# A table of places is changed in a fused two-layer FNet and Infini-attention kernel: natural scores, value products, key, query, value and output chains

## The chip, the cores and the metric

The kernel runs on one core of one Trainium2 chip. The metric is the device time of one execution in microseconds (us), lower is better. The times and the profile are of the whole program: one launch, all inputs and the output in the chip's memory.

Engines are named as the profile names them: PE is TensorE (matmuls; PEld its weight loads), DVE is VectorE, ACT is ScalarE, POOL is GpSimd, SP is SyncE, whose instruction queue issues nearly all the DMAs.

## The reference, cut to what matters

```
x = x + A(layernorm(x))      # A: y = Re(DFT_seq(DFT_hidden(x)))
x = x + B(layernorm(x))      # B: attention in 4 segments with a memory
x = x + A(layernorm(x))
x = x + B(layernorm(x))

# B, with S = 2048 rows, D = 512, 32 heads of 16, segments of L = 512 rows:
q, k, v = x@wq, x@wk, x@wv           # per head
for s in range(4):
    logits = q_s @ k_s.T * scale + mask       # causal in a segment
    a_dot  = softmax(logits) @ v_s
    a_mem  = (phi(q_s) @ M) / (phi(q_s) @ z + 1e-6)
    o_s    = g * a_mem + (1 - g) * a_dot
    M, z   = M + phi(k_s).T @ v_s, z + sum(phi(k_s))
return concat(o) @ wo
```

All numbers are float32; the matmuls of A and the projections of B split each operand into two float32r parts and add three products.

## The kernel before

The four layers follow each other with an overlap: the first layer A runs to about 373 us in the profile, its last step (`y`, the hidden DFT) to about 448 us, the first attention B from about 440 to 900 us, the second A to 1305 us, the second B to the end.

**A unit** of an attention is one segment and four heads; there are 32 in each attention, eight in a segment. A unit's work:

- `stack` loads a unit's queries and keys (`stkq`, `stkk`) by DMA. Two heads stand in the upper and two in the lower half of the 128 rows, so that a matmul of one half and one of the other run side by side.
- `natural_max` makes the scores row by row (`nat`, on PE), and DVE takes each row's maximum out of them (`junk<-nat`, `mx`). It has five steps: 512 columns for the first pair of heads, then 128 and 384, the same again for the second pair, and 256 twice for both. The last step writes the negated maxima (`mparts`).
- `max_rows` turns them over (`mT` on PE, `mt` on ACT) and a DMA puts them beside the queries.
- `softmax_values` makes the scores again, turned (`sT`, on PE), less the maximum, and ACT caps and exponentiates them (`sT<-sT`, `pT<-sT`). It has five steps as well: 256 columns twice, 384 and 128 twice, 512 twice.
- `value_products` multiplies with the values (`pv_bank`), ACT copies the sum (`ot`), and `output` turns it (`on`) and scales it on DVE (`rec`, `ot<-on`).

Between these stands **the chain**: the key, query, value and output projections (`pqk`, `pvv`, `po`) of the neighbouring segments, cut into half products of 64 rows (`half_product`). A tile of the chain takes 12 steps in the upper half of the rows, and 18 steps after its start (`LAGS`) 12 steps in the lower half, so that two tiles in a row overlap and most steps are a pair. A unit has 24 steps: 10, then 6, then 8, each such window spread over a part of the unit (`WIN`). The order of the tiles is a string (`ORDER` for the two middle segments, `ORDER_FIRST`, `ORDER_LAST`), two names for each unit, where `-` is none.

At a unit's head stand, in some units, the memory's reads (`mem_read`: `pm`, with `den` and `onat` on DVE) and updates (`mem_update`: `pkT`, copied by ACT as `pkn`, and `pM`, added up on DVE), the turns of the next segment's rows (`prep`: `xnT`), and of the attention's outputs (`transpose_out`: `oT`).

**What sets the order.** Nothing of this is ordered by a scheduler on PE. Each step is put at a place, a number: unit n begins at place t = t0 + 10n, and the tables say how far from t a step stands (`N_AT` for the natural scores, which run up to 16 places ahead, `S_AT` for the softmax, `PV` for the value products, `TURN` for `max_rows`, and `UPA`, `UPB`, `READ_AT` in units for the memory). All steps are sorted by their place, and PE's instructions keep that order. DVE, ACT, POOL and SP get theirs from the framework, which starts from the same order and knows priorities; the maxima have a high one.

All PE results go to eight banks of 512 numbers per row (`bank`). A new result takes the bank that has been free the longest, and its first matmul waits until DVE or ACT has emptied it.

The lines that the prediction speaks of:

```
1338  place(0, softmax_values(*unit(n)), [t + k for k in sorted(set(S_LAST if light_unit else S_AT))])
1343  place(1.9, max_rows(*unit(n)), [turn])
1344  place(1, natural_max(*unit(n)), [t + k for k in (N_LAST if light_nat else N_AT)])
1374  chain.update({at + h: tile for h, tile in enumerate(order) if tile})
1407          return t0 + SU * u + at + 1.8 * r / n
```

Of the kernel before, what the change touches and what calls it, by code (L numbers as in the profile page):

```python
# [27 lines left out]
LT = L // P  # L28
# [13 lines left out]
VW = DH + 1  # L42
HALF = NT // 2
URGENT = 150
S_AT = (1.0, 2.5, 3, 5.5, 7.5)
N_AT = (-16.05, -15.1, -12.05, -10.95, -8.0, -8)
PV = 11.9
PVF = 12
W = 2.5
TURN = -5  # L50
TO = 0.75
TURNED = (12.5, 12.5, 14)
WIN = ((4.1, 10), (6.1, 6), (8.1, 8))
LAGS = 18
ORDER = "k3 q3 o1 o0 o2 o3 k0 q0 v2 q1 k1 k2 v1 q2 v3 v0"
OT_AT = (1, 1, 1, 2)
PREP_AT = (2, 3)
READ_AT = (1, 3, 5, 7)
UPA = (-1, 3, 3, 7)
UPB = (4, 5, 6, 8)  # L60
ORDER_PRE = "q2 k2"
ORDER_FIRST = "q3 k3 - - - - v2 k0 q0 q1 k1 k2 v0 q2 v3 v1"
PREP_FIRST = (2, 3)
UPA_FIRST = (1, 2, 4, 5)
UPB_FIRST = (2, 7, 8, 8)
ORDER_LAST = "k3 q3 o2 o0 - o3 - o1 - - - - - - - -"
OT_LAST = (1, 2, 1, 1)
READ_LAST = (1, 3, 5, 6)
NL0 = 0
SL0 = 2  # L70
TURN_LAST = -5
TURNED_LAST = (12.5, 12.5, 14)
TO_LAST = 0.8
ROWS_AT = (-38, -24, -12, 2, 26, 28, 40, 66)
S_LAST = (1.5, 2.5, 3, 6.0, 6)
N_LAST = (-15.55, -14.05, -12.5, -11.0, -10.9, -8)
PV_LAST = 11.5
OWO = 0.8
OWU = 0.6
OWP = 0.4  # L80
OWR = 0.2
OWB = 0.3
STK = -21.5
TERMS = {
# [14 lines left out]
def spectral_infini_kernel(  # L99
# [151 lines left out]
    def place(order, gen, *at):  # L251
        for t in itertools.chain(*at):
            slots.setdefault(t, []).append((order, gen))

    def run_from(t, n, step=1):
        return range(t, t + n * step, step)
# [18 lines left out]
    def place_spectral(x_in, x_out, t0, end, ln_at, direct):  # L275
# [340 lines left out]
        def split_u(tcn, tt):  # L616
            sl = slice(tt * P, (tt + 1) * P)
            for cc in range(2):
                home = ("ut", 8) if (tcn, cc) == (TC - 1, 1) else ("w", 16)
                us[tcn, tt, cc] = t = pair("us", *home)  # L620
                for half in range(2):
                    hi, lo = (
                        t[:, h, half * 256 : (half + 1) * 256].rearrange("p (m s) -> p m s", s=P)
                        for h in range(2)
                    )
                    split(hi, lo, c[tcn, (half, cc)][:, :, sl])
            yield
# [72 lines left out]
        else:  # L700
# [25 lines left out]
            for tcns in (0, 1), (2, 3):  # L726
                at = {tcn: [] for tcn in tcns}
# [13 lines left out]
        for tcn in range(TC):  # L741
            if tcn == 0:
                at = [end + k // 2 for k in range(nh)]
            elif tcn < TC - 1:
                at = [end + nh // 2 + ((tcn - 1) * nh + k) // 3 for k in range(nh)]
            else:
                at = run_from(end + nh // 2 + 2 * nh // 3 + 1, 2 * DT, 2)
                at = [*at, *(at[-1] + 4 + k for k in range(LT))]
            for tt in range(LT):
                place(3.7, split_u(tcn, tt), [at[tt * 2 * DT if tcn < TC - 1 else 0] - 4])  # L750
            place(4, (hidden if tcn < TC - 1 else hidden_last)(tcn), at)

    def place_attention(x_in, x_out, t0, w_at, out_at):
# [241 lines left out]
        def max_rows(s, g, u):  # L995
            qs, parts = stacks[s, g, u, "q"], maxima.pop((s, g, u))
            n = MROWS * HU * LT
            mt = sb.tile([P, P], F32R, name="mt", bufs=2)
            for a in SIDES:
                at = slice(a, a + P // 2)  # L1000
                pt = bank("mT", (P, P // 2))
                T.transpose(pt[:MCOLS], parts[at].bitcast(F32), ident[at, at])
                with tc.high_priority(offset=URGENT):
                    A.activation(mt[:n, at], pt[:n], AF.Copy)
            for a, at in enumerate(SIDES):
                n = MROWS * HP * LT
                nc.sync.dma_start(
                    qs[at + KROWS : at + KROWS + MROWS].rearrange("p h s -> p (h s)").bitcast(F32),
                    mt[a * n : (a + 1) * n].bitcast(F32),
                )  # L1010
            yield

        def softmax_values(s, g, u):
# [57 lines left out]
            def ev(t, f):  # L1071
                events.setdefault(t, []).append(f)

            for p in range(HP):
# [13 lines left out]

                ev((S_LAST if (s, g * NU + u) >= (NSEG - 1, SL0) else S_AT)[3 + p], first)
                ev((S_LAST if (s, g * NU + u) >= (NSEG - 1, SL0) else S_AT)[1 + p], second)  # L1090
            p2 = []
# [6 lines left out]

            ev((S_LAST if (s, g * NU + u) >= (NSEG - 1, SL0) else S_AT)[0], third)

# [18 lines left out]
        def value_products(s, g, u):  # L1119
            pending.pop((s, g, u))()  # L1120
            yield
# [191 lines left out]
        def unit(n):  # L1313
            return n // USEG, n % USEG // NU, n % NU
# [15 lines left out]
        def apart(s, k):  # L1330
            return t0 + SS * s + SU * k + W

        for n in range(NSEG * USEG):
# [3 lines left out]
            final = n >= NSEG * USEG - 2  # L1337
            place(0, softmax_values(*unit(n)), [t + k for k in sorted(set(S_LAST if light_unit else S_AT))])
            place(0.9, value_products(*unit(n)), [t + (PVF if final else PV_LAST if light_unit else PV)])
            turned = t + (TURNED_LAST if light_unit else TURNED)[2 if n >= NSEG * USEG - 3 else n % USEG == USEG - 1]  # L1340
            place(TO_LAST if light_unit else TO, output(*unit(n)), [turned])
            turn = t - (6 if x_out is out_tiles and n == NSEG * USEG - 1 else -(TURN_LAST if light_nat else TURN))
            place(1.9, max_rows(*unit(n)), [turn])
            place(1, natural_max(*unit(n)), [t + k for k in (N_LAST if light_nat else N_AT)])
            place(0.6, stack(*unit(n)), [t + STK])
        for s in range(NSEG):
            b = t0 + SS * s
            for j in range(2):
                t = b - 43 + 5 * j if s == 0 else apart(s - 1, (PREP_AT if s > 1 else PREP_FIRST)[j])
                first = (11, 8, 5, 3) if s else (8, 5, 4, 3)  # L1350
                place(OWP, prep(s, (2 * j, 2 * j + 1)), [*(t - d for d in first), t, t + 1] if s == 0 else [*(t - d for d in first), t])
            if s == 0:
# [5 lines left out]
            for i in range(LT):  # L1358
                if s > 0:
                    place(OWO, transpose_out(s - 1, i), [apart(s, (OT_AT if s < NSEG - 1 else OT_LAST)[i])])  # L1360
            order = []
            for name in (ORDER_FIRST if s == 0 else ORDER if s < NSEG - 1 else ORDER_LAST).split():
                n, i = name[0], int(name[1:] or 0)
# [23 lines left out]
            for g in range(NG):  # L1387
# [9 lines left out]
                if s > 0:  # L1397
                    place(OWR, mem_read(s, g), [apart(s, (READ_AT if s < NSEG - 1 else READ_LAST)[g])] * 2)
                if s < NSEG - 1:
                    update = mem_update(s, g)  # L1400
                    place(OWU, update, [apart(s, (UPA if s else UPA_FIRST)[g])])
                    place(OWB, update, [apart(s, (UPB if s else UPB_FIRST)[g])])
        def chain_time(k):
# [23 lines left out]
    b2 = a2 + TC * 7 * HALF + LEAD  # L1427

    def w_at(b):
        return lambda k: b - 52 + 2 * k if k < 12 else b + 20 + 5 * (k - 12)  # L1430

    place_spectral(
        x_tiles, mids[0], a1, b1 - LEAD,
# [5 lines left out]
        mids[1], mids[2], a2, b2 - LEAD,  # L1439
        [((2 * j, 2 * j + 1), a2 + t) for j, t in enumerate(ROWS_AT)],  # L1440
        False,
# [87 lines left out]
```

## Time and profile before

| | us |
|---|---|
| time, median of 3 runs (lowest, highest) | 1762.76 (1760.72, 1765.97) |
| the profiled execution's own time | 1763.62 |
| its span, first to last instruction | 1761.5 |
| PE busy in the span | 1719.8 |
| DVE, ACT, POOL busy | 1315.4, 1092.1, 489.6 |

The profile is of one execution. A busy PE is not PE at its peak: matmuls are pipelined, their ends are modelled, and a gap of under 0.15 us counts as none. So the waits of PE are read from the starts of its rows in the timeline: two rows that stand next to each other without a wait start one matmul's length apart.

### The profile page before, as it was taken

How to read it: one execution, taken by the hardware profiler on the slowest of the kernel's cores; microseconds unless marked ns; L12 is line 12 of the kernel's file. 1: busy time of each engine (PE TensorE's matmuls, PEld its weight loads, DVE VectorE, ACT ScalarE, POOL GpSimd, SP SyncE). 2: the span in 40 equal slices, each digit the busy share in tenths (PEclk: the TensorE clock that was granted, in tenths of full speed). 3: DMA queues.
4: the chain of work that ended last, by engine and by line, in shares of the span. 5: the costliest groups of instructions: out<-in, count | busy, mean ns of one | idle time of the engine just before them, and what ended most of it. 6: DMA issues, size and time to landing. Idle time of an engine off the chain costs nothing.

```text
span 1761.5 us, 35311 instructions
## 1 busy us (share of the span) xinstructions
PE 1719.8 (98%) x11504; PEld 1347.1 (76%) x11504; DVE 1315.4 (75%) x3939; ACT 1092.1 (62%) x2452; POOL 489.6 (28%) x767
## 2 busy tenths in 40 slices
PE   8999999999999999999999999999999999999998
PEld 6888777878677787777678878888876777778775
DVE  8888977873676876878978997667647668677785
ACT  3344443532489788788774566444318887887885
POOL 1000000004237455455410000000034454753542
PEclk9999999999999999999999999999999999999999
DMA  8787774355356454555657767653545555545551
GB/s 283 246 271 236 241 258 163 107 175 176 111 148 163 129 155 110 163 155 149 176 186 227 262 224 243 193 171 117 179 150 155 130 128 158 152 122 155 143 143 34
DMA packets 145510, 303.28 MB, mean 172 GB/s; under 512 B 18096, under 2 KB 22192, under 8 KB 145328
## 3 DMA queue, kind: packets, MB, share of 16 engines
q1 hardware_dynamic: 138416, 288.44, 55.3%
q10 hardware_dynamic: 6912, 12.59, 1.9%
q8 instruction: 93, 1.52, 0.4%
q14 instruction: 89, 0.73, 0.1%
HBM read 211.83 MB, written 88.08 MB: 170 GB/s over the span
## 4 chain that ended last, share of the span: by engine, by line
PE 79%; DVE 10%; ACT 4%; DMA 3%; issue 3%; POOL 0%; SPq 0%; DVEq 0%; ACTq 0%; POOLq 0%
PE m L125 25%; PE pqk L125 9%; PE y L125 8%; PE pv_bank L125 8%; PE nat L125 6%; PE u L125 5%; PE pvv L125 5%; PE po L125 5%; PE sT L125 4%; DVE junk L969 2%; DVE c L592 2%; DVE clo L142 1%; PE pM L125 1%; ACT pT L1043 1%; PE pm L125 1%
## 5 line engine op out<-in xcount | busy, mean ns | idle before, releaser
L969 DVE CUSTOM_DVE_ANT_0 junk<-nat,mask 128x128 bf16<-128x128 f32 (+3 forms) x896 | 368.7, 457 | 226.2 <-PE nat L125 214.2
L1043 ACT ACTIVATE pT<-sT 128x512 f32<-128x512 f32 x640 | 352.2, 608 | 2.5 <-DVE sT L1038 1.3
L125 PE MATMUL m<-chi,xa 128*128 128x512 f32 x1056 | 308.2, 392 | 2.4 <-DVE c L592 2.1
L1046 POOL TENSOR_SCALAR_AFFINE_SELECT pT<-pT 128x256 f32<-128x256 f32 (+1 forms) x448 | 192.3, 443 | 336.5 <-ACT pT L1043 298.7
L125 PE MATMUL m<-clo,xa 128*128 128x512 f32 x720 | 231.3, 393 | 5.0 <-DVE clo L142 4.7
L125 PEld LDWEIGHTS m<-chi,xa 128*128 128x128 f32 x1056 | 198.1, 189 | 46.5 <-DVE c L592 2.9
L1040 ACT ACTIVATE sT<-sT 128x256 f32<-128x256 f32 x625 | 180.0, 329 | 72.3 <-PE sT L125 63.9
L125 PE MATMUL nat<-stkk,stkq 48*128 48x384 f32 (+3 forms) x1024 | 195.3, 356 | 8.6 <-PE sT L125 3.1
L125 PE MATMUL pqk<-xT,wq 64*128 64x512 f32 (+1 forms) x720 | 194.1, 402 | 0.8 <-ACT pT L1043 0.6
L125 PE MATMUL pqk<-xT,wk 64*128 64x512 f32 (+1 forms) x720 | 193.8, 398 | 0.2
L125 PE MATMUL y<-wdt,us 128*128 128x512 f32 x768 | 182.4, 391 | 0.2 <-DVE wdt L142 0.2
L125 PE MATMUL pvv<-wv,xT 64*128 64x512 f32 (+1 forms) x672 | 175.1, 402 | 0.6 <-DVE xT L142 0.6
L125 PEld LDWEIGHTS nat<-stkk,stkq 48*128 48x128 f32 x1024 | 123.5, 189 | 60.7 <-ACT pT L1043 19.3
L125 PEld LDWEIGHTS y<-wdt,us 128*128 128x128 f32 x768 | 143.5, 188 | 30.5 <-DVE wdt L142 0.9
L125 PE MATMUL pv_bank<-pT,v_all 128*32 128x512 f32 (+3 forms) x2048 | 164.1, 453 | 0.6 <-DVE xr L236 0.6
L125 PE MATMUL sT<-stkq,stkk 50*128 50x256 f32 (+3 forms) x1024 | 163.2, 332 | 1.1 <-DVE mx L969 0.4
L125 PEld LDWEIGHTS m<-clo,xa 128*128 128x128 f32 x720 | 135.1, 188 | 38.0 <-DVE clo L142 9.4
L211 POOL TENSOR_TENSOR r<-ve,half_neg 128x4 f32<-128x4 f32 (+2 forms) x22 | 20.8, 945 | 510.4 <-DVE ve L209 486.5
L140 ACT ACTIVATE chi<-cring 128x512 fp32r<-128x512 f32 (+1 forms) x138 | 99.7, 728 | 89.5 <-PE m L125 42.4
L125 PE MATMUL po<-wo,oh 64*128 64x512 f32 (+1 forms) x672 | 145.9, 398 | 1.3 <-ACT oh L140 0.5
L125 PEld LDWEIGHTS pqk<-xT,wq 64*128 64x128 f32 (+1 forms) x720 | 125.8, 190 | 12.9 <-issue 1.5
L125 PEld LDWEIGHTS pqk<-xT,wk 64*128 64x128 f32 (+1 forms) x720 | 122.8, 186 | 12.2 <-issue 2.2
(191 smaller groups left out, 3124.3 us busy)
## 6 DMA issues: line engine op xcount, KB each, us to landing
cring<-in_ct SPq DMA_DIRECT2D x97, 256.0 KB
scrk<-parts SPq DMA_DIRECT2D x96, 256.0 KB
stkq<-scrq SPq DMA_DIRECT2D x128, 192.0 KB
stkk<-scrk SPq DMA_DIRECT2D x128, 192.0 KB
cring<-sum SPq DMA_DIRECT2D x95, 256.0 KB
xt<-mid SPq DMA_DIRECT2D x64, 256.0 KB
scrq<-parts SPq DMA_DIRECT2D x32, 512.0 KB
cring<-in_ct SPq DMA_DIRECT2D x27, 512.0 KB
```

What stands on the lines that cost most here:

```text
L125: return tc.keep_in_program_order(op(*args, **kwargs))
L140: pin(A.activation(hi, src, AF.Copy, scale=scale))
L142: lo_engine.tensor_tensor(out=lo, in0=src, in1=hi.bitcast(F32), op=ALU.subtract)
L211: G.tensor_tensor(out=r, in0=ve, in1=half_neg[:, :n], op=ALU.pow)
L592: V.tensor_tensor(out=dst, in0=c[tcn, base][:, m], in1=ps[m], op=op)
L969: last_max[0] = V.tensor_tensor_reduce(trash, src, mask[:, 512 - n :], 1.0, 3e38, ALU.add, ALU.min, dst,)
L1040: done = A.activation(blocks, blocks, AF.Relu)
L1043: A.activation(dst[a], ps, AF.Exp, scale=-SCALE)
L1046: G.affine_select(blocks, blocks, pattern=[[0, n] for n in blocks.shape[1:-1]] + [[1, P]], compare_op=ALU.is_ge, fill=0.0, base=0, channel ...
```

## The change

The change is in constants and in two expressions that now read theirs from constants. `N_AT` puts the first two natural steps a place later, `S_AT` and `PV` the first softmax step and the value products half a place sooner, `READ_AT`, `UPA`, `UPB` the memory's reads and updates to other units; `ORDER` exchanges the first two tiles and the order of the values; `ORDER_LAST` and `READ_LAST` put the last segment's output tiles elsewhere; `WO` and `WOS` place the loads of the output weights; `ROWS_AT` those of the second layer A's rows. `MDELAY` is 4, as it was.

```
-S_AT = (1.0, 2.5, 3, 5.5, 7.5)
-N_AT = (-16.05, -15.1, -12.05, -10.95, -8.0, -8)
-PV = 11.9
+S_AT = (0.5, 2.5, 3, 5.5, 7.5)
+N_AT = (-15.05, -14.15, -12.0, -10.95, -8.0, -8)
+PV = 11.5
-TO = 0.75
+TO = 0.7
-ORDER = "k3 q3 o1 o0 o2 o3 k0 q0 v2 q1 k1 k2 v1 q2 v3 v0"
+ORDER = "q3 k3 o1 o0 o2 o3 k0 q0 v1 q1 k1 k2 v2 q2 v0 v3"
-READ_AT = (1, 3, 5, 7)
-UPA = (-1, 3, 3, 7)
-UPB = (4, 5, 6, 8)
+READ_AT = (1, 2, 5, 7)
+UPA = (1, 3, 3, 6)
+UPB = (3, 4, 6, 8)
-UPA_FIRST = (1, 2, 4, 5)
-UPB_FIRST = (2, 7, 8, 8)
-ORDER_LAST = "k3 q3 o2 o0 - o3 - o1 - - - - - - - -"
+UPA_FIRST = (1, 1, 3, 5)
+UPB_FIRST = (2, 8, 8, 7)
+ORDER_LAST = "k3 q3 o0 o2 - - - o1 - o3 - - - - - -"
-READ_LAST = (1, 3, 5, 6)
+READ_LAST = (1, 1, 5, 6)
+MDELAY = 4
+WO = 25
+WOS = 4
-ROWS_AT = (-38, -24, -12, 2, 26, 28, 40, 66)
-S_LAST = (1.5, 2.5, 3, 6.0, 6)
-N_LAST = (-15.55, -14.05, -12.5, -11.0, -10.9, -8)
+ROWS_AT = (-38, -26, -18, 2, 26, 26, 40, 66)
+S_LAST = (1.5, 2.5, 3, 5.5, 6)
+N_LAST = (-15.05, -14.55, -12.0, -11.0, -10.9, -8)
-OWO = 0.8
+OWO = 0.85
-OWP = 0.4
-OWR = 0.2
+OWP = 0.3
+OWR = 0.1
...
-                at = [*at, *(at[-1] + 4 + k for k in range(LT))]
+                at = [*at, *(at[-1] + MDELAY + k for k in range(LT))]
...
-        return lambda k: b - 52 + 2 * k if k < 12 else b + 20 + 5 * (k - 12)
+        return lambda k: b - 52 + 2 * k if k < 12 else b + WO + WOS * (k - 12)
```

What PE gets of it in a unit of a middle segment, before. It is the first attention's unit that starts at 597.8 us in the profile, whose chain is outputs alone (`po`); rows with x10 are five pairs:

```order
L125 MATMUL sT<-stkq,stkk 128x384 x2
L125 MATMUL sT<-stkq,stkk 128x128 x2
L125 MATMUL nat<-stkk,stkq 128x512 x2
L125 MATMUL po<-wo,oh 128x512 x10
L125 MATMUL nat<-stkk,stkq 128x128 x2
L125 MATMUL nat<-stkk,stkq 128x384 x2
L125 MATMUL mT<-ident,mparts_71 72x64 x2
L125 MATMUL po<-wo,oh 128x512 x6
L125 MATMUL sT<-stkq,stkk 128x512 x2
L125 MATMUL po<-wo,oh 128x512 x14
L125 MATMUL sT<-stkq,stkk 128x512 x2
```

And the same stretch of the same unit now:

```order
L128 MATMUL sT<-stkq,stkk 128x384 x2
L128 MATMUL sT<-stkq,stkk 128x128 x2
L128 MATMUL po<-wo,oh 128x512 x10
L128 MATMUL nat<-stkk,stkq 128x512 x2
L128 MATMUL mT<-ident,mparts_71 72x64 x2
L128 MATMUL po<-wo,oh 128x512 x6
L128 MATMUL sT<-stkq,stkk 128x512 x2
L128 MATMUL po<-wo,oh 128x512 x4
L128 MATMUL nat<-stkk,stkq 128x128 x2
L128 MATMUL nat<-stkk,stkq 128x384 x2
L128 MATMUL po<-wo,oh 128x512 x10
L128 MATMUL sT<-stkq,stkk 128x512 x2
```

The first natural step (512 columns) has gone behind five pairs of the chain, and the second (128 and 384) behind five pairs and the first `sT` of 512 columns; `mT` now stands right behind the first natural step. So it is in every unit that has a chain.

What DVE gets in that unit, before, from the copy of the turned rows (`xT`) on. An `ISA` row with an input is a maximum, and the trace calls it CUSTOM_DVE_ANT_0:

```order
L142 TENSOR_TENSOR oh<-oT,oh 128x512
L969 ISA junk,mx<-nat,mask 128x128
L969 ISA mx 128x1
L969 ISA junk,mx<-nat,mask 128x384
L969 ISA mx 128x1
L969 ISA junk,mx<-nat,mask 128x128
L969 ISA mx 128x1
L236 TENSOR_TENSOR xr<-po,xr 128x512
L969 ISA junk,mx<-nat,mask 128x384
```

And now:

```order
L145 TENSOR_TENSOR oh<-oT,oh 128x512
L239 TENSOR_TENSOR xr<-po,xr 128x512
L201 BN_STATS st<-xr 128x6
L202 BN_AGGR row_mv<-st 128x2
L972 ISA junk,mx<-nat,mask 128x128
L972 ISA mx 128x1
L972 ISA junk,mx<-nat,mask 128x384
L972 ISA mx 128x1
```

The maxima of the second natural step now stand behind the sum and the row statistics of a finished output tile.

What PE gets in the last unit before the second layer A's matmuls (it starts at 854.7 us), before, from its second `sT` on:

```order
L125 MATMUL nat<-stkk,stkq 128x512 x2
L125 MATMUL mT<-ident,mparts_70 72x64 x2
L125 MATMUL nat<-stkk,stkq 128x128 x2
L125 MATMUL nat<-stkk,stkq 128x384 x2
L125 MATMUL sT<-stkq,stkk 128x512 x4
L125 MATMUL nat<-stkk,stkq 128x512 x2
```

And now:

```order
L128 MATMUL nat<-stkk,stkq 128x512 x2
L128 MATMUL mT<-ident,mparts_70 72x64 x2
L128 MATMUL po<-wo,oh 128x512 x2
L128 MATMUL nat<-stkk,stkq 128x128 x2
L128 MATMUL nat<-stkk,stkq 128x384 x2
L128 MATMUL sT<-stkq,stkk 128x512 x2
L128 MATMUL po<-wo,oh 128x512 x2
L128 MATMUL sT<-stkq,stkk 128x512 x2
L128 MATMUL po<-wo,oh 128x512 x6
L128 MATMUL nat<-stkk,stkq 128x512 x2
```

This unit had no chain; it now has the lower half of the last output tile, 12 steps.

## The prediction

> **What bounds the kernel now.** I read the page's busy times first, then the chain of work that ended last, then PE's timeline unit by unit.
>
> ```profile
> PE 1719.8 (98%) x11504; PEld 1347.1 (76%) x11504; DVE 1315.4 (75%) x3939; ACT 1092.1 (62%) x2452; POOL 489.6 (28%) x767
> ...
> PE 79%; DVE 10%; ACT 4%; DMA 3%; issue 3%; POOL 0%; SPq 0%; DVEq 0%; ACTq 0%; POOLq 0%
> ```
>
> PE is in a matmul for 98% of the span, and 79% of the last chain is PE. So PE bounds the program, but the busy share hides what can be won: 13% of the chain is DVE and DMA, and a PE row that waits for its bank counts as busy while the rows ahead of it drain. Since the change removes no matmul, only such waits, and stretches at a low clock, can go. The windows of the eight units of a middle segment (segment 1 of the first attention) show how unequal they are:
>
> ```profile
> 582.40:597.80 15.40, 15.08 (x140) 11.42 (x138) 11.23 (x49) 13.12 (x33) 7.60 (x11) 1.00 0.39 102
> ...
> 682.80:695.40 12.60, 12.60 (x130) 10.01 (x129) 8.18 (x38) 10.37 (x26) 7.50 (x12) 1.00 0.51 123
> sum 113.00, PE 111.27 PEld 87.98 DVE 85.50 ACT 93.67 POOL 63.88; mean PE 13.91 PEld 11.00 DVE 10.69 ACT 11.71 POOL 7.99
> ```
>
> First and last of eight: 15.40 and 12.60 us. Most of the difference is work (reads, updates and turns at the head), and no engine but PE is full. The waits are found by starts, in the stretch that the change rearranges: from the second `sT` row to the 128-column `nat` row.
>
> ```profile
> 588.18 0.62 PE L125 MATMUL sT<-stkq,stkk 50*128 50x384 f32 x4
> ...
> 591.12 0.48 PE L125 MATMUL nat<-stkk,stkq 48*128 48x128 f32 x4
> ...
> 646.76 0.50 PE L125 MATMUL sT<-stkq,stkk 50*128 50x384 f32 x4
> 647.33 0.80 PE L125 MATMUL nat<-stkk,stkq 48*128 48x512 f32 x2
> ...
> 649.09 0.47 PE L125 MATMUL nat<-stkk,stkq 48*128 48x128 f32 x4
> ...
> 687.31 0.50 PE L125 MATMUL sT<-stkq,stkk 50*128 50x384 f32 x4
> 687.64 0.45 PE L125 MATMUL nat<-stkk,stkq 48*128 48x512 f32 x2
> 687.93 0.40 PE L125 MATMUL pqk<-xT,wk 64*128 64x512 f32 x1
> ...
> 689.08 0.51 PE L125 MATMUL nat<-stkk,stkq 48*128 48x128 f32 x4
> ```
>
> The last unit (687.31) has no wait: `sT` takes 0.33, `nat` of 512 columns 0.29, and five pairs 689.08 - 687.93 = 1.15, so 0.23 a pair; 1.77 us in all. The first (588.18 to 591.12) takes 2.94, the one at 646.76 takes 2.33. In order, the eight lie above 1.77 by 1.17, 1.39, 0.25, 0.44, 0.56, 0.02, 0.41 and 0.02: **4.26 us in a segment**. What they wait for is a bank. In the unit at 646.76:
>
> ```profile
> 646.81 0.75 DVE L1187 TENSOR_TENSOR onat<-pm,den 128x256 f32<-128x256 f32 x2
> 647.48 0.29 DVE L1220 TENSOR_TENSOR pkn<-pM,same_head 128x136 f32<-128x136 f32 x1
> ```
>
> DVE empties the banks of `pm` at 647.56 and that of `pM` at 647.77; `nat` and the first pair cannot run before. The other causes are alike: banks of the turned rows and outputs that DVE or ACT still copies, and in two units queries or keys whose DMA lands late.
>
> **The change, part by part.** Edit one, `N_AT`: behind the second `sT` row now stand five pairs (1.15 us), whose banks are mostly held already by tiles begun earlier; `nat` of 512 columns comes 1.15 us later, `mT` right behind it, and `nat` of 128 and 384 behind the first `sT` of 512. A wait of `nat` for a bank that is freed up to 1.15 us after its old place goes, so all of the 4.26 could. I do not take all. A chain step starts a new tile in some units and then needs a bank itself; and where the memory is read, DVE's row from `onat` to `ot<-on` is the same, so the next row on PE that needs what DVE frees meets it a little later. I keep the two reading units (0.56 and 0.41), 0.25 in the second unit (one of its two causes) and 0.55 in the first (`xT` of the next rows): 1.77 kept, 4.26 - 1.77 = 2.5 us gone.
>
> New costs of the same edit. First, seven pairs lie between the two `sT` of 512 columns, now with the `nat` of 128 and 384 among them, which takes the banks that stood free; so the second `sT` needs the bank that the first's exponentials free. Where a key or query tile ends in the unit, ACT is late (PE's rows, then ACT's):
>
> ```profile
> 663.02 0.40 PE L125 MATMUL sT<-stkq,stkk 50*128 50x512 f32 x2
> ...
> 665.33 1.00 PE L125 MATMUL nat<-stkk,stkq 48*128 48x512 f32 x2
> ```
> ```profile
> 662.82 0.60 ACT L897 ACTIVATE praw<-pqk 128x512 f32<-128x512 f32 x1
> ...
> 665.18 1.09 ACT L1043 ACTIVATE pT<-sT 128x512 f32<-128x512 f32 x2
> ```
>
> That `sT` stands at 663.02, and half of its exponentials are done at 665.18 + 0.6 = 665.78, 2.76 us later, since the key tile's copies begin at 662.82. PE would come 2 x 0.23 + 0.29 + 5 x 0.23 + 0.23 = 2.13 us later: a wait of 0.63. Bounds: 0 (the old order has its wait a few rows later: the `nat` row of 665.33 takes 1.00 where the one of 687.64 takes 0.45, and the new wait may only replace it) and 0.63; I take 0.2, nearer to the lower since the replaced wait is in the same trace, in 3 of 8 units: 0.6. Second, in output units DVE's maxima of the second natural step now stand behind the output sum and the statistics:
>
> ```profile
> 608.27 0.69 DVE L236 TENSOR_TENSOR xr<-po,xr 128x512 f32<-128x512 f32 x1
> ...
> 609.80 0.68 DVE L198 BATCH_NORM_STATS2 st<-xr 128x6 f32<-128x512 f32 x1
> ```
>
> They hold two banks for up to 0.69 + 0.68 = 1.37 us longer (0 if the other banks suffice); I take 0.5 in each of the two output units with most DVE work: 1.0. A middle segment wins 2.5 - 0.6 - 1.0 = 0.9; there are two in each attention, four in all: **3.6 us**.
>
> The first segments have the same stretch without outputs:
>
> ```profile
> 532.83 0.81 PE L125 MATMUL sT<-stkq,stkk 50*128 50x384 f32 x3
> ...
> 535.44 0.48 PE L125 MATMUL nat<-stkk,stkq 48*128 48x128 f32 x4
> ```
>
> 2.61 us, 0.84 above 1.77, of which 0.1 is a late matmul of `sT` itself; three units of the segment lose about 0.7 each in this way, 2.1 us. DVE has no output sums here, so I keep 0.3 and pay 0.4 (0.2 in two units with a key or query tile): 1.4 in each of two, **2.8 us**.
>
> Edit two, `ORDER_LAST`: the last segment's output tiles take other places. The four units from 820 us on had 24, 18, 12 and 0 chain steps, and get 18, 12, 18 and 12, six more in all (less overlap of two tiles), 6 x 0.23 = 1.4 us of PE work. The last of them is the one with nothing to fill it:
>
> ```profile
> 854.70:863.80 9.10, 6.84 (x65) 4.28 (x64) 9.05 (x41) 6.65 (x17) 2.93 (x7) 1.00 1.03 300
> 863.90:870.70 6.80, 6.55 (x33) 3.51 (x35) 6.68 (x27) 5.46 (x14) 2.54 (x6) 0.50 0.52 177
> 1724.10:1730.90 6.80, 6.64 (x47) 3.12 (x45) 6.08 (x31) 3.08 (x6) 1.88 (x5) 0.50 0.00 1
> ```
>
> PE idles 9.10 - 6.84 = 2.26 us there, and its granted clock is 0.50 for the 6.80 us behind it; at full clock the 6.55 busy us of that window would take about half, so the dip costs up to 3.3. The new steps (12 x 0.23 = 2.76 us) lie in the idle time: I take 0.7 won for the fill in each attention (2.1 hidden of the 2.76, less the 1.4 that is new) and, in the first, 2.5 of the 3.3 for the dip. The second attention's dip (1724.10) comes in the tail, where chain steps hardly reach; I leave it. Sum **3.9 us**.
>
> [...]
>
> Edits at nothing. The later loads of the output weights: first used a segment later, behind which all of PE's work of that time hides them. The second layer A's rows and the moved write of `mid`: SP's queue issues them among other loads; the nearest row for one that is late is the chain's
>
> ```profile
> 1491.14 5.50 DMA out<-xr
> ```
>
> so 0 to 5.5 us, and I take 0, since the loads that PE needs next were issued ahead. `UPA`, `UPB`, `READ_AT` move the same matmuls and DVE rows between heads: the 0.97 of the reading units stays, in other units; between -1 and +1 a segment, taken at 0. `MDELAY` is as it was, and `S_AT`'s first entry, `PV` and `TO` move no row on PE.
>
> **Sum.** 3.6 + 2.8 + 3.9 = 10.3 us. The profiled execution took 1763.6 (a span of 1761.5 and 2.1 around it), so 1753.3 for one like it; the median of the runs is 0.9 lower, and I forecast **1752.5** on that scale. Ends: all stretch waits gone (4 x 4.26 + 2 x 2.1 = 21.2), both dips (6.6) and 2 of fill, 30 us, 1733; only new costs, 4 x 1.6 + 2 x 0.4 = 7.2, 1770.
>
> **Rivals.** (a) *The waits only change place.* Five pairs later DVE is still the one that frees the head's banks, and `nat`, `mT` or the third window's `sT` waits as long. For it: DVE's rows at the head are unchanged. Against: two of eight units wait for nothing now, so banks suffice when the head is light. The gain then is the fill (1.4), less some of the new costs: about 1762. 20 in 100.
>
> (b) *Nearly all goes*, the stretch waits and edit two's term, with new costs of 3 to 7: 21.2 + 3.9 - 5 = 20, about 1743. For it: the causes end 0.3 to 1.2 us after the old place, within the 1.15 of five pairs. Against: the new orders on DVE. 12 in 100.
>
> (c) *New stretches at half clock* in the units at 820 and 833, which lose chain steps: each 6.80 us window at 0.50 costs 3.3, two of them 6.6, so 1759. Against: PE is busy without long gaps there now. [...] 7 in 100.
>
> (d) *Slower: `mT` waits.* It stands right behind the first `nat`, 0.33 + 1.15 + 0.24 = 1.72 us after the second `sT` row. The bank that it takes next may be one of that `sT`, which ACT empties late:
>
> ```profile
> 647.89 1.10 ACT L1043 ACTIVATE pT<-sT 128x512 f32<-128x512 f32 x2
> ```
>
> Its second exponential ends at 648.99, 2.23 us after the row at 646.76. If that bank is taken, PE stops for 0.5, and everything behind `mT` with it: 32 units of the middle segments x 0.5 = 16 us, against the 10.3 won: 1762.8 - 10.3 + 16 = about 1769. It decides once ACT ends later than 1.72 us after the row in most units. Against: the first exponential's bank is free at 1.73, and the five pairs leave other banks. 14 in 100.
>
> **How the numbers follow.** The forecast has 47 in 100 (wins of 6 to 17 us). Faster by over 0.3% (5.3 us, about what a measurement of this kernel can tell from no change): 47 + 12 = 59. Within it: (a) and (c), 27. Slower: (d), 14. The range reaches from 1739, which takes in most of (b) and its lower new costs, to 1766, which takes in (a), (c) and the milder part of (d); beyond it lie the rest of (b) and most of (d), some 15 in 100. The forecast's own range is 1746 to 1757.
>
> **What would show it.** Right: the eight stretches of segment 1, measured now from the second `sT` row over five pairs to the end of the first `nat`, lie above 1.77 by 1.8 in sum; the window behind the last unit has a clock near 1.00; the second `sT` of 512 waits under 0.3 us in three units. Wrong: `nat` or `mT` starts over 0.4 us after the row ahead of it in most units (a, d); a clock of 0.50 in the units from 820 us (c); DVE's busy share in output units at its full, with `nat` of 128 and 384 waiting for banks.

## The result, and the profile after

| | us |
|---|---|
| changed kernel, median of 4 runs (lowest, highest) | 1746.04 (1743.35, 1753.72) |
| kernel before beside it, median of 4 runs | 1762.84 |
| ratio, with its 95% interval | 0.9907 [0.9891, 0.9924] |
| the profiled execution: time, span | 1743.35, 1741.5 |

The change is **16.8 us faster**; 10.3 were forecast, and the time lies in the range. In the changed kernel every line number is higher by three. The page of the changed kernel, busy times and the chain of work that ended last:

```profile
PE 1701.1 (98%) x11504; PEld 1327.2 (76%) x11504; DVE 1316.4 (76%) x3939; ACT 1088.5 (63%) x2452; POOL 490.2 (28%) x767
...
PE 80%; DVE 10%; ACT 4%; issue 4%; DMA 1%; POOL 1%; SPq 0%; DVEq 0%; ACTq 0%; POOLq 0%
```

DVE, ACT and POOL are as busy as before; PE, with the same 11504 matmuls, is busy for 18.7 us less. So nothing was taken away, and PE's rows last shorter: they wait less for banks, and fewer of them run at half clock (both are shown below). Both parts have to be told apart, and the table below does it by stage. A unit is counted from the first row of its value products to that of the next unit, in the two profiled executions.

| stage, us in the profiled execution | before | after | difference | forecast |
|---|---|---|---|---|
| up to the first unit | 476.7 | 472.8 | -3.9 | 0 |
| first segments (two of 8 units) | 105.6, 105.3 | 101.9, 102.8 | -6.2 | -2.8 |
| middle segments (four of 8 units) | 113.0, 110.2, 113.0, 110.1 | 111.2, 109.7, 110.6, 108.3 | -6.5 | -3.6 |
| last segments (the first with the second A, the second to PE's last row) | 535.0, 88.3 | 533.4, 86.5 | -3.3 | -3.9 |

Of the 3.9 us ahead of the first unit, up to 3.4 are the clock: the trace of before has two stretches at half clock there (at 273.4 and 468.0 us, 3.4 us each), the one of the change none. The one at 273.4 doesn't come from PE's order: up to 434 us PE has the same rows in the same order in both kernels.

The windows of the eight units of segment 1 of the first attention, PE's busy time first and the granted clock third from the end:

```profile
574.70:590.50 15.80, 15.16 (x144) 11.33 (x142) 11.89 (x50) 14.07 (x34) 8.06 (x13) 1.00 0.40 103
...
673.40:685.90 12.50, 12.50 (x128) 9.43 (x126) 8.81 (x40) 10.39 (x27) 7.61 (x12) 1.00 0.55 127
sum 111.20, PE 109.21 PEld 83.74 DVE 85.59 ACT 93.44 POOL 63.88; mean PE 13.65 PEld 10.47 DVE 10.70 ACT 11.68 POOL 7.99
```

They sum to 111.2 where before had 113.0. The unit that the prediction read, the fifth of the segment, from its second `sT` row in PE's timeline:

```profile
638.92 0.50 PE L128 MATMUL sT<-stkq,stkk 50*128 50x384 f32 x4
639.26 0.44 PE L128 MATMUL pqk<-xT,wk 64*128 64x512 f32 x1
...
640.47 0.39 PE L128 MATMUL nat<-stkk,stkq 48*128 48x512 f32 x2
640.70 0.45 PE L128 MATMUL mT<-ident,mparts 64*72 64x64 f32 x2
```

From `sT` to the row behind `nat` (640.70) it is 1.78 us, so the 0.56 of before are gone. DVE still empties the banks of `pm` at the head; its `pkn` row isn't in this unit any more, since the change moved that update to another one:

```profile
639.48 0.75 DVE L1190 TENSOR_TENSOR onat<-pm,den 128x256 f32<-128x256 f32 x2
```

`onat` ends at 640.23, past the old place of `nat`, but beside the five pairs now, whose banks are held already. The moved update isn't the reason: in e1 below, with `N_AT` alone, this unit still has `pkn` (from 644.18 on), and the stretch from `sT` at 643.90 to the row behind `nat` at 645.65 takes 1.75 us.

A second wait went that the prediction didn't see. The 32 matmuls of the value products, before (597.83) and now, in the second unit of the segment:

```profile
597.83 2.83 PE L125 MATMUL pv_bank<-pT,v_all 128*32 128x512 f32 x32
```
```profile
590.52 2.36 PE L128 MATMUL pv_bank<-pT,v_all 128*32 128x512 f32 x32
```

0.47 us less. Before, one of them starts at 597.83 and the next ones only from 598.27 on, where now four start at once. One of DVE's maxima ends at 598.26 (597.71 + 0.55), so a bank is the likely cause; no run tries it by itself. Summed by starts over the four middle segments: the stretch, from the first `sT` row on, -9.5 us, the value products -2.9, everything behind the stretch +4.9, and the heads, with rows that moved in, +1.0.

New is a wait of the second `sT` of 512 columns, as forecast. PE, then ACT, in the unit that starts at 647.0:

```profile
654.59 0.39 PE L128 MATMUL sT<-stkq,stkk 50*128 50x512 f32 x2
...
656.71 0.39 PE L128 MATMUL sT<-stkq,stkk 50*128 50x512 f32 x1
657.41 0.49 PE L128 MATMUL sT<-stkq,stkk 50*128 50x512 f32 x1 [0.31 <-ACT pT L1046]
```
```profile
656.75 1.09 ACT L1046 ACTIVATE pT<-sT 128x512 f32<-128x512 f32 x2
```

PE arrives 2.12 us after the first `sT` (2.13 was worked out). The first half of the pair finds a bank; the other waits until half of the exponentials are done, 657.41 instead of 656.94, so 0.47 us.

**The clock.** The granted clock of the changed kernel's trace is 0.50 in three stretches:

```profile
493.20:500.00 6.80, 6.80 (x42) 3.77 (x41) 6.09 (x23) 4.33 (x11) 1.46 (x4) 0.50 0.83 220
831.10:837.90 6.80, 6.80 (x33) 4.36 (x35) 6.44 (x28) 3.84 (x8) 5.00 (x7) 0.50 0.90 202
...
1349.90:1356.70 6.80, 6.65 (x42) 3.76 (x44) 5.50 (x22) 3.76 (x11) 1.45 (x3) 0.50 0.91 237
```

20.4 us in all. The trace of before has seven stretches of 3.4 or 6.8 us, 37.5 us. In the second of the three, `po` rows that follow each other start 0.43 us apart (at 834.05, 834.47 and 834.90) where a pair of the chain took 0.23 at full clock. So nearly half of PE's time is lost there, and at a half, by this estimate, up to 8.5 us of the 20.0 by which the two spans differ are the clock. The mean clock is given for each run, so this share can be taken out: **time less (1 - clock) x span**, called the net time below. The clock has three digits, which leaves about 0.9 us open.

### The profile page after: what moved, and what is told of

Read it like the earlier page. It is cut to its first block, busy times and chain, and to the rows that moved or that the text cites. A ratio compares the mean times of both kernels' runs of the same rounds, so it can differ in the third digit from the quotient of the medians.

```text
span 1741.5 us, 35374 instructions
## 1 busy us (share of the span) xinstructions
PE 1701.1 (98%) x11504; PEld 1327.2 (76%) x11504; DVE 1316.4 (76%) x3939; ACT 1088.5 (63%) x2452; POOL 490.2 (28%) x767
## 4 chain that ended last, share of the span: by engine, by line
PE 80%; DVE 10%; ACT 4%; issue 4%; DMA 1%; POOL 1%; SPq 0%; DVEq 0%; ACTq 0%; POOLq 0%
PE m L128 26%; PE pqk L128 9%; PE y L128 8%; PE pv_bank L128 8%; PE pvv L128 5%; PE nat L128 5%; PE sT L128 4%; PE po L128 4%; PE u L128 4%; DVE junk L972 2%; DVE c L595 2%; DVE clo L145 1%; PE pM L128 1%; ACT pT L1046 1%; PE on L128 1%
## 5 line engine op out<-in xcount | busy, mean ns | idle before, releaser
L128 PE MATMUL pqk<-xT,wq 64*128 64x512 f32 (+1 forms) x720 | 198.5, 397 | 0.4 <-DVE mx L972 0.4
L128 PE MATMUL nat<-stkk,stkq 48*128 48x384 f32 (+3 forms) x1024 | 179.6, 344 | 2.8 <-ACT pT L1046 0.8
L128 PE MATMUL sT<-stkq,stkk 50*128 50x256 f32 (+3 forms) x1024 | 167.0, 334 | 6.4 <-ACT pT L1046 3.3
L128 PEld LDWEIGHTS m<-clo,xa 128*128 128x128 f32 x720 | 134.7, 188 | 38.3 <-DVE clo L145 10.1
L128 PE MATMUL pv_bank<-pT,v_all 128*32 128x512 f32 (+3 forms) x2048 | 157.6, 447 | 0.6 <-DVE mx L972 0.2
L128 PE MATMUL po<-wo,oh 64*128 64x512 f32 (+1 forms) x672 | 155.5, 402 | 2.5 <-DVE oh L145 1.5
L128 PEld LDWEIGHTS nat<-stkk,stkq 48*128 48x128 f32 x1024 | 117.4, 187 | 43.4 <-ACT pT L1046 16.2
L128 PEld LDWEIGHTS sT<-stkq,stkk 50*128 50x128 f32 x1024 | 104.9, 186 | 42.5 <-ACT pT L1046 10.2
```

The costliest lines, as they stand in the source:

```text
L128: return tc.keep_in_program_order(op(*args, **kwargs))
```

## The experiments

All are runs beside the kernel before, which took 1762 to 1763 us (median) at a clock of 0.990, net 1743 to 1745. The clock and the net time are medians over a kernel's runs.

| run | median us | ratio to before | clock | net us |
|---|---|---|---|---|
| the change | 1746.04 | 0.9907 [0.9891, 0.9924] | 0.9925 | 1732.8 |
| e1, `N_AT` alone | 1752.88 | 0.9949 [0.9936, 0.9962] | 0.989 | 1733.7 |
| e2, memory's places alone | 1776.56 | 1.0075 [1.0062, 1.0088] | 0.988 | 1754.3 |
| e3, last segment's tables alone | 1774.51 | 1.0063 [1.0048, 1.0077] | 0.9835 | 1745.8 |
| e4, change without `N_AT` | 1784.17 | 1.0126 [1.0112, 1.0139] | 0.986 | 1759.5 |
| e5, change without memory's places | 1751.73 | 0.9935 [0.9923, 0.9947] | 0.991 | 1734.5 |
| e6, change without last segment's | 1747.94 | 0.9917 [0.9904, 0.9929] | 0.990 | 1730.5 |
| e7, first natural step alone | 1780.12 | 1.0108 [1.0093, 1.0123] | 0.986 | 1756.8 |
| e8, change, second step sooner | 1746.41 | 0.9918 [0.9904, 0.9931] | 0.993 | 1733.9 |
| e9, the same in 7 of 32 units | 1750.93 | 0.9928 [0.9910, 0.9946] | 0.990 | 1733.8 |
| e10, change, first segments' old places | 1754.44 | 0.9947 [0.9933, 0.9961] | 0.9885 | 1734.0 |
| e11, change, old loads and `ORDER` | 1756.15 | 0.9963 [0.9952, 0.9975] | 0.985 | 1730.7 |
| e12, the change again | 1746.43 | 0.9912 [0.9894, 0.9930] | 0.9915 | 1732.0 |

### e1: `N_AT` alone

```diff
-N_AT = (-16.05, -15.1, -12.05, -10.95, -8.0, -8)
+N_AT = (-15.05, -14.15, -12.0, -10.95, -8.0, -8)
```

> The kernel before with the new N_AT alone: in every unit with a chain the first natural step stands behind five pairs and the second behind the first sT of 512; nothing else is changed. Theory A (the waits at banks behind the second sT row go, as the prediction had it): the waits in that stretch, 31.4 us over all units by the starts in the trace of before, fall to about 17, new waits of about 3 at the second sT of 512 come, and the time falls by 8 to 12 us beside before. Rival B (the memory's reads and updates in other units make the gain): within 4 us of before. Rival C (the difference is stretches at half clock, which come by chance): time less the share lost to the clock, (1 - mean granted clock) x span, is within 3 us of before's 1744.2.

9.4 us faster, net 10.1 (1743.8 to 1733.7). The waits in the stretch fell from 17.1 to 11.0 us in the four middle segments (7.6 in the change), and the value products take 18.3 us in each of them as in the change (18.8 to 19.3 before), so their gain is `N_AT`'s as well. Theory A holds, B and C fall: the net time of this one edit is already within 1 us of the whole change's.

### e2: the memory's places alone

```diff
-READ_AT = (1, 3, 5, 7)
-UPA = (-1, 3, 3, 7)
-UPB = (4, 5, 6, 8)
-UPA_FIRST = (1, 2, 4, 5)
-UPB_FIRST = (2, 7, 8, 8)
+READ_AT = (1, 2, 5, 7)
+UPA = (1, 3, 3, 6)
+UPB = (3, 4, 6, 8)
+UPA_FIRST = (1, 1, 3, 5)
+UPB_FIRST = (2, 8, 8, 7)
```

> The kernel before with READ_AT, UPA, UPB, UPA_FIRST and UPB_FIRST of the change alone: the same reads and updates at the heads of other units. Theory A: between 1 us slower and 3 us faster than before, as the same rows move from one head to another. Rival B: 8 us faster or more, and the units that start at 641 and 669 us in the profile of before are 1.5 us shorter each.

14.3 us slower: both theories fall. The middle segments lose 14.8 us, 10.1 of them in their second units. Such a unit now reads the memory and also turns the next rows; it takes 17.53, 17.30, 17.28 and 17.73 us, where before had 14.9 each time. One of them (it starts at 712.6, all at full clock), PE and then DVE:

```profile
719.11 0.80 PE L128 MATMUL sT<-stkq,stkk 50*128 50x384 f32 x4 [0.17 <-DVE onat L1190]
719.95 0.49 PE L128 MATMUL nat<-stkk,stkq 48*128 48x512 f32 x1
720.68 0.47 PE L128 MATMUL nat<-stkk,stkq 48*128 48x512 f32 x1 [0.23 <-DVE xT L145]
...
722.37 0.46 PE L128 MATMUL nat<-stkk,stkq 48*128 48x128 f32 x4
```
```profile
718.54 0.76 DVE L1190 TENSOR_TENSOR onat<-pm,den 128x256 f32<-128x256 f32 x2
719.22 0.68 DVE L145 TENSOR_TENSOR xT<-xnT,xT 128x512 fp32r<-128x512 f32 x1
...
719.89 0.68 DVE L145 TENSOR_TENSOR xT<-xnT,xT 128x512 fp32r<-128x512 f32 x1
```

DVE has `onat` and two copies of turned rows in its queue, 2.0 us from 718.54 to 720.57, and each empties a bank. `nat` stands right behind `sT` and waits for them: 3.26 us from `sT` to the second `nat` step instead of 1.77. In the changed kernel the same unit has the same reads and turns at its head:

```profile
707.56 0.66 PE L128 MATMUL sT<-stkq,stkk 50*128 50x384 f32 x4
708.25 1.43 PE L128 MATMUL po<-wo,oh 64*128 64x512 f32 x10
709.50 0.41 PE L128 MATMUL nat<-stkk,stkq 48*128 48x512 f32 x2
709.73 0.41 PE L128 MATMUL mT<-ident,mparts 64*72 64x64 f32 x2
```

709.73 - 707.56 = 2.17 us, 0.40 above 1.77, because the five pairs come first. So the crowded head costs 1.49 us without the five pairs and 0.40 with them.

### e3: the last segment's tables alone

```diff
-ORDER_LAST = "k3 q3 o2 o0 - o3 - o1 - - - - - - - -"
+ORDER_LAST = "k3 q3 o0 o2 - - - o1 - o3 - - - - - -"
-READ_LAST = (1, 3, 5, 6)
+READ_LAST = (1, 1, 5, 6)
-S_LAST = (1.5, 2.5, 3, 6.0, 6)
+S_LAST = (1.5, 2.5, 3, 5.5, 6)
-N_LAST = (-15.55, -14.05, -12.5, -11.0, -10.9, -8)
+N_LAST = (-15.05, -14.55, -12.0, -11.0, -10.9, -8)
```

> The kernel before with ORDER_LAST, READ_LAST, S_LAST and N_LAST of the change alone: the last segment of each attention. The prediction's term: 3.9 us faster, 2.5 of them a stretch at half clock behind the unit at 854.7 that goes. Rival by the result's trace (the seven units from 805 us took as long after as before, 99.4 us in both, and a stretch at half clock stood 20 us earlier): within 2 us of before in the first attention, some 2 us faster in the second; 0 to 3 us faster in all.

12.2 us slower, but only 2.0 net: the rest is the clock, with stretches at half clock of 10.2, 3.4 and 13.7 us one after the other from 827 us on, and 10.2 at 1732. Neither expectation held. The first of the stretches begins in the first of the units that lost chain steps, as rival (c) of the prediction had it.

### e4: the change without `N_AT`

> The changed kernel with N_AT of before: all the rest of the change. Theory A: 8 to 12 us slower than the changed kernel's 1746, so 1754 to 1758. Rival B: within 4 us of the changed kernel. Rival C: its time less (1 - clock) x span is within 3 us of the changed kernel's 1733.

The edit is that of e1, undone in the changed kernel. 38 us slower than the changed kernel, three times the most that Theory A allowed, and 22 slower than before. `N_AT` is worth 9.4 us in the old surroundings and 38 in the new ones (net 10.1 and 26.7): **the edits don't add**.

### e5 and e6: the change without the memory's places, and without the last segment's tables

The edits of e2 and of e3, undone in the changed kernel.

> The changed kernel with READ_AT, UPA, UPB, UPA_FIRST and UPB_FIRST of before. The new N_AT alone was 9.4 us faster than before, these places alone 14.3 slower. Theory A (the places pay only where N_AT lets the head's waits go: the units at 634 and 661 us in the changed profile, 0.7 us each below those of N_AT alone): 3 to 6 us slower than the changed kernel's 1746. Rival B (the places always cost): 3 us faster than it or more. Rival C (only stretches at half clock differ): time less (1 - clock) x span stays at 1733, within 2 us.

5.7 us slower than the changed kernel: Theory A's size. But net only 1.7 (1734.5 to 1732.8), so B falls and C holds: most of what the places win beside `N_AT` is clock.

> The changed kernel with ORDER_LAST, READ_LAST, S_LAST and N_LAST of before. Alone they were 12 us slower, 10 of them in the first attention's last segment, where stretches at half clock came. Theory A (with N_AT that segment's clock holds up): 2 to 5 us slower than the changed kernel's 1746. Rival: within 2 us of it or faster.

1.9 us slower by the medians, with intervals that overlap (0.9904 to 0.9929 and 0.9891 to 0.9924): not told apart from nothing. Net it is 2.3 faster (1.5 beside the second set of runs of the change, e12). So the last segment's tables seem to cost some 2 us of work or waits and to return them in clock; single runs of one kernel spread over 5 us net, so the size is loose.

### e7: the first natural step alone

```diff
-N_AT = (-16.05, -15.1, -12.05, -10.95, -8.0, -8)
+N_AT = (-15.05, -15.0, -12.05, -10.95, -8.0, -8)
```

> The kernel before with only the first natural step a place later (-15.05, and the second right behind it at -15.0): behind the second sT row stand five pairs, then both natural steps, then mT. Theory A (the first step's waits for banks are what N_AT removes; the second step's new place is what makes the second sT of 512 wait by 0.4 us in 20 units): 9 to 14 us faster than before, and the second sT of 512 waits no more. Rival B (two natural steps in a row want three banks at once, and the wait moves to the second): within 5 us of before.

18.2 us slower than before: both theories fall, and rival (d) of the prediction appears. Behind the five pairs stand now both natural steps and then `mT`, in the unit that starts at 646.9; PE, then DVE:

```profile
654.52 0.92 PE L128 MATMUL nat<-stkk,stkq 48*128 48x512 f32 x6
655.20 0.22 PE L128 MATMUL mT<-ident,mparts 64*72 64x64 f32 x1
655.71 0.24 PE L128 MATMUL mT<-ident,mparts 64*72 64x64 f32 x1 [0.28 <-DVE mx L972]
```
```profile
654.95 0.69 DVE L972 CUSTOM_DVE_ANT_0 junk<-nat,mask 128x512 bf16<-128x512 f32 x1 [0.32 <-PE nat L128]
```

It looks as if the natural steps have taken the free banks; the second `mT` gets the one whose maximum DVE has just found (ending at 655.64). The groups by line give the idle time of PE ahead of `mT` in the whole program behind the last bar (the sum, then its parts by what ended it), here and in the changed kernel:

```profile
L128 PE MATMUL mT<-ident,mparts 64*72 64x64 f32 x128 | 27.5, 235 | 15.4 <-DVE mx L972 10.9 <-DVE oh L145 1.5 <-DVE rt L220 1.4
```
```profile
L128 PE MATMUL mT<-ident,mparts 64*72 64x64 f32 x128 | 21.9, 224 | 2.3 <-ACT pT L1046 1.1 <-DVE oh L145 0.3 <-DVE ot L1153 0.3
```

15.4 against 2.3 us, 10.9 of the 15.4 ended by DVE's maxima. So both moves of `N_AT` are needed: the first step behind the five pairs, and the second away from it, behind the first `sT` of 512.

### e8 and e9: the second natural step ahead of the first `sT` of 512

```diff
-N_AT = (-15.05, -14.15, -12.0, -10.95, -8.0, -8)
+N_AT = (-15.05, -14.6, -12.0, -10.95, -8.0, -8)
```

> The changed kernel with the second natural step at -14.6 in place of -14.15: it stands ahead of the first sT of 512 and not two pairs behind it. Theory A (the second sT of 512 waits by 0.40 to 0.48 us in some 20 units since the second natural step takes the free banks between the two): 4 to 8 us faster than the changed kernel. Rival B (the banks are short either way, and the first sT of 512 or the natural step waits instead): within 3 us of it, or slower.

The same time as the changed kernel (1746.41, net 1733.9). The wait of the second `sT` is gone, in the unit that starts at 648.9:

```profile
656.77 0.40 PE L128 MATMUL sT<-stkq,stkk 50*128 50x512 f32 x2
658.61 0.41 PE L128 MATMUL sT<-stkq,stkk 50*128 50x512 f32 x2
```

1.84 us apart, seven pairs and the `sT` itself. It is paid elsewhere: the units at 635.7 and 662.1 are 0.63 and 0.66 us longer than in the changed kernel, those at 648.9 and 622.4 are 0.47 and 0.75 shorter. Rival B. e9 takes the sooner place only in the units that had won by it:

```diff
-[t + k for k in (N_LAST if light_nat else N_AT)]
+[t + k for k in (N_LAST if light_nat else N_SOON if n in SOON else N_AT)]
+N_SOON, SOON = (-15.05, -14.6, -12.0, -10.95, -8.0, -8), (7, 8, 11, 14, 16, 19, 22)
```

> The changed kernel with the second natural step at -14.6 (ahead of the first sT of 512) in seven of the 32 units of each attention, the ones whose interval was shorter in the run with -14.6 throughout, and at -14.15 in the rest. Theory A (each unit's waits depend on its own head and tiles, so the better place can be taken unit by unit): the sum of those units' differences, 3.0 and 3.1 us in the two attentions, so 6 us below the changed kernel, some 1740. Rival B (the units are coupled through the order in which banks come free, so what one wins the next one loses): within 2 us of the changed kernel.

Rival B again: net 1733.8. In segment 1 the first and the sixth unit are 0.42 and 0.45 shorter, and the second, fifth and seventh, which run the same rows on PE as in the changed kernel, 0.68, 0.66 and 0.64 longer; the fourth, which took the sooner place too, won nothing. The wait is handed on, by banks or by ACT, whose rows changed order as well; which of them wasn't tried.

### e10: the first segments' old places in the changed kernel

```diff
-UPA_FIRST = (1, 1, 3, 5)
-UPB_FIRST = (2, 8, 8, 7)
+UPA_FIRST = (1, 2, 4, 5)
+UPB_FIRST = (2, 7, 8, 8)
```

> The changed kernel with UPA_FIRST and UPB_FIRST of before: the first segments' updates at the old heads, the middle segments' places as changed. The stretch at half clock that stood at 507 us in the runs with the old places and the new N_AT (6.8 us long) and not in the changed kernel: Theory A (it comes from the first segment's old places): it is back, and the time is 3.5 to 6 us above the changed kernel's. Rival B (it comes by chance, or from the middle segments' places): no stretch at 507, and within 2 us of the changed kernel.

8.4 us slower, net 1.2: Theory A by the stretch, though the time is 2.4 us beyond its most. The stretch at half clock is back; the window of e10, then the one of the changed kernel at that place:

```profile
507.40:514.20 6.80, 6.80 (x28) 5.38 (x28) 4.40 (x16) 3.58 (x9) 0.81 (x2) 0.50 0.52 136
```
```profile
506.80:513.60 6.80, 6.80 (x67) 4.78 (x68) 5.08 (x22) 4.73 (x12) 1.45 (x3) 1.00 0.68 167
```

It stands in all four profiles with the first natural step at its new place and the first segments' old places (e1, e5, e7, e10), in none of the six with both new (the change, e6, e8, e9, e11, e12), and in none of the four with the old `N_AT` (before, e2, e3, e4). So these two lines, taken at nothing by the prediction, take away a stretch that the new `N_AT` brings. `N_AT` takes two away itself: 8 to 11 us ahead of the first unit of each attention (at 468.0 and 1331.5 us before) a stretch of 3.4 or 6.8 us begins in all four profiles with the old `N_AT` and in none of the other ten. The rest of the 8.4 is more clock: a stretch of 10.2 us at 1692 that the first profile of the change hasn't.

### e11: old loads and `ORDER`

```diff
-ORDER = "q3 k3 o1 o0 o2 o3 k0 q0 v1 q1 k1 k2 v2 q2 v0 v3"
+ORDER = "k3 q3 o1 o0 o2 o3 k0 q0 v2 q1 k1 k2 v1 q2 v3 v0"
-WO = 25
-WOS = 4
+WO = 20
+WOS = 5
```

and `ROWS_AT`, `OWO`, `OWP`, `OWR` of before.

> The changed kernel with ORDER, WO, WOS, ROWS_AT, OWO, OWP and OWR of before. The prediction took these edits at nothing: within 2 us of the changed kernel. Rival (a late transfer of a row or of the output weights, 5.5 us at most): 2 to 6 us slower or faster, in the units near 1480 us or at the start of the second layer A.

10.1 us slower than the changed kernel and 2.1 faster net (1.3 beside e12): no late transfer is to be seen, and the two attentions' first and middle segments take 0.6 us less in sum than in the changed kernel. The clock is 0.981 to 0.988 in its ten runs. Two of the stretches, in the last segment of the second attention:

```profile
1694.00:1704.20 10.20, 10.20 (x44) 6.86 (x46) 6.52 (x32) 5.21 (x14) 2.71 (x7) 0.50 0.44 105
1721.30:1731.50 10.20, 10.20 (x59) 5.91 (x57) 6.72 (x30) 3.68 (x8) 2.16 (x5) 0.50 0.07 27
```

Every engine runs the same rows in the same order there as in the changed kernel, but for PE's rows that start side by side, yet the stage took 95.3 us instead of 86.5.

### e12: the changed kernel again

> The changed kernel once more, nothing edited. In all traces so far the stretches at half clock begin and end on a grid of 3.413 us that stands elsewhere in each execution. Theory A (which stretches come in the last segments is a matter of where that grid falls, so the same program has them at other places in another execution): the stretch of 6.8 us at 831 us is not found again at the same place in this profile, the single times spread over 1743 to 1754 again, and every time less (1 - clock) x span lies within 1730 to 1736. Rival B (the program alone sets them, and the edits of the loads and orders removed 10 us of them for good): stretches at 493, 831 and 1350 us as before, clock 0.993 or more in nearly all runs, and a median of 1743 to 1746.

Theory A, with the one stretch in the first segment (493 us) found again in both. The windows at half clock of this execution:

```profile
493.40:500.20 6.80, 6.80 (x40) 4.05 (x42) 6.45 (x25) 4.68 (x14) 1.81 (x4) 0.50 0.80 214
821.10:831.30 10.20, 10.20 (x58) 5.85 (x57) 7.16 (x31) 4.14 (x11) 2.79 (x5) 0.50 0.62 159
1353.60:1357.00 3.40, 3.40 (x25) 1.59 (x25) 3.40 (x15) 1.70 (x5) 0.78 (x2) 0.50 1.00 234
1705.10:1715.30 10.20, 10.20 (x56) 5.96 (x55) 7.08 (x33) 3.57 (x8) 2.37 (x6) 0.50 0.07 28
```

The middle segments repeat to 0.2 us each (111.2, 109.7, 110.4, 108.3), and the tail's stage takes 90.8 instead of 86.5, with a stretch at 1705 that the first profile hadn't. Its six runs spread from 1744 to 1752 at clocks of 0.988 to 0.994, and net they lie within 1730.0 and 1734.0.

What can't be told by these runs: why e11's clock is lower in all ten runs, since chance alone would have given it runs like e12's. `ORDER` and the loads weren't tried apart. `S_AT`, `PV` and `TO` weren't run by themselves either.

## Why the prediction was right, and where it was off

- **What bounds the kernel: right.** PE has the same rows, and the gain is waits and clock alone.
- **The stretch behind the second `sT`: right, and its size too, but partly by luck.** 2.5 us in a middle segment were to go; the four lost 2.5, 1.9, 2.7 and 2.4. The units differ from the forecast: the fifth and the seventh, which read the memory, kept nothing though 0.97 was kept for them, since `onat` now ends beside the pairs. The first two kept 0.91 and 0.41 (0.55 and 0.25 forecast), and the fourth of segment 1, for which nothing was kept, 0.65: 2.0 us in sum there, where 1.8 was the prediction's own sign of being right. The prediction had read that one too low: from its first `sT` row at 631.72 to `nat` at 634.21 it lies 0.72 above 1.77, not 0.44, and the segment's sum is some 4.5.
- **The new costs: right in sum.** 1.6 a middle segment forecast, 6.4 in four; behind the stretch stand 4.9 more. The second `sT` waits 0.40 to 0.48 where 0.2 was taken and 0.63 worked out. That it is a cost by itself isn't shown: e8 takes it away and the time stays.
- **Not seen: the value products' waits**, 2.9 us in the middle segments. This is the term missing in the middle segments, 6.5 measured for 3.6. In the first segments, 6.2 for 2.8, the stretch gave 2.1 of the 3.6 forecast for it; the value products gave 1.1, the heads, with one update fewer, 0.8, and the rows behind the stretch 2.2 where 0.8 of new costs was forecast. Alone, `N_AT` is worth 10.1 us net where 6.4 was forecast.
- **`ORDER_LAST`: wrong.** 3.9 us was forecast, with the dip behind 863.9 gone and the second attention's kept. In the change the tables' part isn't told from nothing (1.9 us). Two steps failed. The fill, taken at 1.4 us won, didn't come: net the tables cost 2.0 alone (e3) and some 2 beside the rest (e6). And filling the one idle unit doesn't simply lift the clock: six steps were taken from each of two units ahead of it, the dip behind it is gone, and a stretch begins in those two units instead, at 831 or 821 us. Rival (c) had that. That filling an idle stretch lifts the clock behind it, for which the forecast took 2.5 us, was the author's estimate, and no run shows it by itself: PE was busy for 2.76 of the 3.41 us ahead of the stretch at 831.1, and e3 shows the price when nothing offsets it, 10 us.
- **The memory's places at nothing: wrong.** "Between -1 and +1 a segment" missed that they depend on `N_AT`: +14.3 us alone, -5.7 beside it, of which 1.7 net and the rest the clock's, with the stretch at 507 us.
- **Loads and `ORDER` at nothing: right net** (the change is 1 to 2 us slower by them), wrong by the clock, 10 us, for a reason that stays open.
- **Rival (d), `mT` waits: right that it can, wrong in what for.** It didn't come in the change, where one natural step stands ahead of `mT` and the wait is 2.3 us in all. With both ahead (e7) it is 15.4, near the 16 worked out, but mostly for DVE's maxima and not for ACT's exponentials.
- **The sum.** Net, the change wins 11 to 13 us, almost all by `N_AT`; the other 4 or 5 are the clock's, 0.990 before and 0.992 now. 10.3 stood for 7.8 of waits and fill and 2.5 of clock: the right direction, each part some two thirds or half of what came. That the clock's term came near is luck: it comes from several edits, the one credited with it costs 10 us of clock alone and returns some beside the others, and single runs of one kernel differ by more. The 16.8 measured is only just inside the forecast's own 6 to 17.

## What to carry to other kernels

Where an engine runs in order and its results share a few banks, put work whose banks are held already behind a crowded head, and what needs new banks after it (0.40 us of wait for 1.49 in the unit shown under e2); then the head can be loaded more, which without it costs more than it wins. Judge edits of an order together: the same places were 14 us slower alone and 6 faster in company. Take the clock's share out of each run before comparing variants that differ by less than 1%: ten runs of one kernel spread over 10 us, and 5 net.

## What the runs showed of the hardware that wasn't expected

Stretches at half clock begin and end on a grid of 3.413 us. In the traces of before and of the change the clock's records at 0.50 last 3413 or 6827 ns, but for a last one that the trace's end cuts off, and in that of before they begin 57, 66, 173, 310, 319 and 425 such lengths behind the first (1450.665 us for the 425, so 3.4133 each). Stretches of 10.2 and 13.7 us in other runs (e3, e11, e12) are three and four lengths. The grid's start against the program differs from execution to execution: what is left of the start of a stretch, divided by 3.4133 us, is 0.34 us in the trace of before, 1.66 in that of the change, 2.2 in e10. So one program can have other stretches in another execution, as the change and e12 do. What sets a stretch off isn't shown: PE was busy for 2.76 of the 3.41 us ahead of the one at 831.1, with no idle piece over 0.5 us.
